# The bias of 739 exps, given as a constant in the instruction instead of by pointer

## The chip, the cores and the metric

The kernel runs on one core of one Trainium2 chip. The metric is the device time of one execution in microseconds (us), the median of several executions. The core has five engines with instruction streams of their own: TensorE (PE in the profile, with its weight loads as PEld), VectorE (DVE), ScalarE (ACT), GpSimd (POOL) and SyncE (SP, which here issues DMA transfers). They meet only at semaphores.

## The reference

Two independent attention blocks with 2048 tokens, width 640 and 32 heads of 20 columns are computed, and their outputs are laid side by side. Block A is softmax attention, block B is linear attention.

```python
# A
scores = jnp.einsum("bhqd,bhkd->bhqk", q, k) * (Dh ** -0.5)
p = _softmax(scores, axis=-1)
o = jnp.einsum("bhqk,bhkd->bhqd", p, v)
# B
phi = lambda t: jnp.where(t > 0, t + 1, jnp.exp(t)) + 1e-6
pq, pk = phi(q), phi(k)
kv = jnp.einsum("bhsd,bhse->bhde", pk, v)
num = jnp.einsum("bhqd,bhde->bhqe", pq, kv)
```

Block A needs 32 x 2048 x 2048 exponentials. Block B needs 2 x 2048 x 640.

## The kernel before, in words

The scores of A are computed transposed, in tiles of 128 keys by 512 queries of one head; one tile is a "unit" and fills one PSUM bank. Eight groups of four heads times four chunks of 512 queries make 32 blocks, each of 16 key tiles times 4 heads.

ScalarE does most of the exponentials. Units are taken in groups of three and two in turn (banks 0 to 2, and banks 3 and 4): `emit_scores` (L1227) issues the score matmuls of group j+1, then `emit_exp` (L1242) issues one ACTIVATE over all banks of group j, so that the scores of one group are computed beside the exp of the other. A group of three is an instruction of 1536 columns, a group of two one of 1024. The result goes as bf16 into the ring `f_PT` of 20 units, from where `emit_pv` (L1368) takes four at a time as moving data of the matmuls with V. In all there are 739 such exps.

VectorE does the remaining units of A by a polynomial on the bits of the number (L1286, L1297, L1301, L1305, into `f_PD`). That form gives the exponential times two to the power 42 (`OCT = 42`) times a small correction (`EXP_S`). ScalarE's exps must carry the same factor, because both kinds of unit are summed together, and it cancels in the normalization. So they add (42 + EXP_S) ln 2 = 29.11 to the exponent: `bias=self.ebias[:, 0:1]`, a column of 128 fp32 numbers in SBUF, which GpSimd fills once at the start (L1035). The scale, 20 to the power -1/2, is a constant in the instruction.

ScalarE has 52 more exps, those of block B (L1554, in `phi`), with scale 1 and bias 0; these carry no tile for the bias. The projections of A, the whole of B, the normalization and the output projections are issued between the exps as background steps.

The order of all instructions on all engines is fixed when the program is built, by a planner (`_Clock`, L728) that keeps an estimated time for each engine. It books `0.062 + 0.4267 * n` us for an exp of n units (L1254), so 1.342 and 0.915 us, and adds a margin `LAG = 0.2` us before results of VectorE and GpSimd count as ready. `bg` (L981) issues background matmuls until TensorE's estimated end reaches the exp's estimated end. `zeros` (L1189) and `fill` (L1208) add matmuls with a zero operand (`f_z`, `f_g`), which change no sum, and whose only effect is that TensorE stays occupied: `fill` does so as long as TensorE's occupied share in the last `SPAN = 3.41` us, weighted by the part of the array that is used, is below `FLOOR = 1.45` us.

Of the kernel before, what the change touches and what calls it, by code (L numbers as in the profile page):

```python
# [5 lines left out]
F32 = mybir.dt.float32  # L6
# [718 lines left out]
LN2 = 0.6931471805599453  # L725
# [74 lines left out]
class _Fast:  # L800
# [53 lines left out]
    def alloc(self):  # L854
        S, NT = self.S, self.NT
        self.KT = self.sb("f_KT", [128, 2, S], BF16)
        self.Qr = self.sb("f_Qr", [128, 4, 512], BF16)
        self.V = self.sb("f_V", [128, NT, N_HEADS, 21], BF16)
        self.xT = self.sb("f_xT", [128, N_DC, S], BF16)
        self.wA = self.sb("f_wA", [128, N_DC, 3 * D_MODEL], BF16)  # L860
        self.wo = self.wA[:, :, 2 * D_MODEL:3 * D_MODEL]
        self.wo7 = self.sb("f_wo7", [128, D_MODEL], BF16)
        self.PT = self.sb("f_PT", [128, self.NPT, 512], BF16)
        self.PD = self.sb("f_PD", [128, self.NPD, 512], BF16)
        self.W = self.sb("f_W", [128, 2, 1024], F32)
        self.PL = self.sb("f_PL", [128, 2, 1024], F32)
        self.T1 = self.sb("f_T1", [128, 512], F32)
        self.Tn = self.sb("f_Tn", [128, 512], BF16)
        self.OTp = self.sb("f_OTp", [128, 512], BF16)
        self.R = self.sb("f_R", [128, 32], F32)  # L870
        self.OTd = self.sb("f_OTd", [128, N_DC, S], BF16)
        self.stage = self.sb("f_st", [128, 4, D_MODEL], BF16)
        self.wBq = self.sb("f_wBq", [128, N_DC, D_MODEL], BF16)
        self.wBkv = self.sb("f_wBkv", [128, N_DC, 2 * D_MODEL], BF16)
        self.woB = self.wBkv[:, :, 0:D_MODEL]
        self.pqT = self.wBkv[:, :, D_MODEL:D_MODEL + 512]
        self.xBt = self.sb("f_xB", [128, 2, N_DC, 512], BF16)
        self.xB = [self.xBt[:, k] for k in range(2)]
        self.kvm = self.sb("f_kvm", [128, N_DC, 21 * N_HEADS], BF16)
        self.kvx = self.sb("f_kvx", [128, 2688 + 10 * 168 + 5 * 168], BF16)  # L880
        self.va = self.kvx[:, 0:2688].rearrange("p (t h j) -> p t h j", t=4, j=21)
        self.kvacc = self.kvx[:, 2688:4368].bitcast(F32).rearrange("p (c n) -> p c n", c=N_DC)
        self.mask = self.kvx[:, 4368:5208].rearrange("p (c n) -> p c n", c=N_DC)
        self.part = self.kvx[:, 0:5120].bitcast(F32).rearrange("p (k n) -> p k n", k=8)
        self.pko = self.sb("f_pk", [128, 4 * D_MODEL], BF16)
        self.pk = self.pko[:].rearrange("p (t n) -> p t n", t=4)
        self.o = self.pko[:, 0:2 * D_MODEL].rearrange("p (t n) -> p t n", t=2)
        self.oT = self.pko[:, 2 * D_MODEL:4 * D_MODEL].rearrange("p (t c m) -> p t c m", t=2, c=N_DC)
        self.ex = self.sb("f_ex", [128, 2, 512], F32)
        self.r1 = self.sb("f_r1", [128, 2, 512], F32)  # L890
        self.rd = self.sb("f_rd", [128, 2, 2, 16], F32)
        self.Z = self.sb("f_z", [128, 128], BF16)
        self.G = self.sb("f_g", [128, 128], BF16)
        self.ebias = self.sb("f_eb", [128, 1], F32)
        self.gmx = self.sb("f_gmx", [128, 2], F32)
        self.ident = self.sb("f_id", [128, 128], BF16)
        self.flag = self.sb("f_flag", [128, 1], I32)
        self.bmx = self.sb("f_bmx", [128, 1], F32)
        self.warm = self.sb("f_warm", [128, 1], F32)
        self.ones = self.sb("f_ones", [128, 1], F32)  # L900
# [115 lines left out]
    def start_loads(self):  # L1016
        sch = self.sch
        awq = self.Aw.rearrange("(c p) n -> p c n", p=128)
        x2 = self.Ax[0]
        xn = self.stage  # L1020
        M = D_MODEL
        for k in range(2):
            sch.dma("sp", lambda e, k=k: e.dma_start(
                xn[:, 2 * k:2 * k + 2, :], x2[256 * k:256 * (k + 1), :].rearrange("(t p) d -> p t d", p=128)),
                writes=tuple(("xn", t) for t in (2 * k, 2 * k + 1)), cost=(0.1, 3.5))
        parts = ((0, 92, ("wq", 0)), (M, M + 92, ("wk", 0)), (2 * M, 2 * M + 160, ("wv", 0)),
                 (M + 92, 2 * M, ("wk", 1)), (92, M, ("wq", 1)), (2 * M + 160, 3 * M, ("wv", 1)))

        def load(q, part):
            a, b, res = part  # L1030
            sch.dma(q, lambda e: e.dma_start(self.wA[:, :, a:b], awq[:, :, a:b]), writes=(res,),
                    cost=(0.5, 5.0 if b - a < 200 else 8.0))
        sch.op("dve", lambda e: e.memset(self.warm[:], 0.0), writes=("warm",))
        sch.op("dve", lambda e: e.memset(self.OTp[:], 1.0), writes=("OTp",), cost=0.3)
        sch.op("pool", lambda e: e.memset(self.ebias[:], (self.OCT + self.EXP_S) * LN2), writes=("ebias",), cost=0.1)  # L1035
        sch.op("act", lambda e: e.activation(self.warm[:], self.warm[:], AF.Exp), writes=("warm",), cost=1.5)
        load("act", parts[0])
        load("act", parts[1])
        load("sp", parts[2])
        for tc in range(1, self.NQC):  # L1040
            for c in range(N_DC):
                sch.dma("sp", lambda e, c=c, tc=tc: e.dma_start_transpose(
                    self.xT[:, c, 512 * tc:512 * (tc + 1)], x2[512 * tc:512 * (tc + 1), 128 * c:128 * (c + 1)]),
                    writes=(("xT", c, tc),), cost=(1.65, 2.0))
        for part in parts[3:]:
            load("sp", part)
# [195 lines left out]
    def emit_exp(self, j):  # L1242
        sch, ps = self.sch, self.ps
        grp = self.groups[j]
        b0 = self.SB[j % 2][0]
        u0 = self.ustart[j]
        s0 = u0 % self.NPT
        n = len(grp)
        assert u0 + n - 1 - self.NPT < 4 * self.pvnext
        scale = float(D_HEAD) ** -0.5  # L1250
        sch.op("act", lambda e: e.activation(self.PT[:, s0:s0 + n, :], ps[:, b0:b0 + n, :], AF.Exp,  # L1251
                                             bias=self.ebias[:, 0:1], scale=scale),
               reads=tuple(("ps", b0 + k) for k in range(n)) + ("ebias",),
               writes=tuple(("PT", s0 + k) for k in range(n)), cost=0.062 + 0.4267 * n)  # L1254

    def d_ready(self, slack):
# [773 lines left out]
```

## Time and profile before

| what | value |
|---|---|
| median of 3 executions | 968.85 us (965.14 to 972.59) |
| the profiled execution's own time | 971.29 us |
| its span, first to last instruction | 969.1 us |
| mean granted TensorE clock | 0.932 of full |
| ScalarE busy | 930.4 us, 96% of the span |
| TensorE busy | 789.4 us, 81% |
| VectorE busy | 718.5 us, 74% |
| GpSimd busy | 160.0 us, 17% |

Busy time is the union of an engine's records. Records of neighbouring instructions on ScalarE overlap, so a record's length is not the time that the instruction costs the engine; that time is the distance from one start to the next. "Idle before" is the time between the end of the records before and the start, and what is named behind it is what ended the wait.

### The profile page before, as it was taken

To read this page: it belongs to the slowest core of one execution; us is meant where nothing else is said; L and a number is where in the kernel's file an instruction comes from. 1 tells how busy PE (TensorE), PEld (TensorE's weight loads), DVE (VectorE), ACT (ScalarE), POOL (GpSimd) and SP (SyncE) were. 2 spreads that over 40 slices of the span, in tenths; PEclk is the share of its full clock that TensorE was granted. 3 is DMA by queue.
4 is the path that set the end of the run, shared out by engine and by line. 5 is a ranking of instruction groups with operands and counts; after the bars stand their busy time and mean duration, and the time that the engine had idled before them with its cause. 6 is when DMAs were issued, how large, how long until landed. Compare 5 with 4: busy or idle time off the path is not lost.

```text
span 969.1 us, 24342 instructions
## 1 busy us (share of the span) xinstructions
PE 789.4 (81%) x10943; PEld 244.1 (25%) x10943; DVE 718.5 (74%) x1003; ACT 930.4 (96%) x799; POOL 160.0 (17%) x154
## 2 busy tenths in 40 slices
PE   8888878777888978787787888887878878878886
PEld 3322222122122222222223122222222222223332
DVE  6768876678789686578885877777887588765773
ACT  6999999999999999999997999999999999999996
POOL 3011301000023121222120320014000310130000
PEclk9989899999889799999998789999998999999999
DMA  6900010000100100100003000010000100000011
GB/s 126 248 5 4 5 32 4 2 5 5 38 5 11 22 5 5 32 5 1 5 5 68 2 3 5 19 43 8 1 12 18 39 6 23 11 5 25 26 40 65
DMA packets 45742, 23.93 MB, mean 25 GB/s; under 512 B 33984, under 2 KB 44992, under 8 KB 45632
## 3 DMA queue, kind: packets, MB, share of 16 engines
q1 hardware_dynamic: 44176, 21.92, 9.6%
q8 instruction: 87, 1.43, 0.6%
q10 hardware_dynamic: 1456, 0.40, 0.2%
q14 instruction: 23, 0.19, 0.1%
HBM read 7.31 MB, written 5.24 MB: 13 GB/s over the span
## 4 chain that ended last, share of the span: by engine, by line
ACT 82%; PE 14%; issue 2%; DVE 1%; ACTq 0%; DVEq 0%
ACT f_PT L1251 80%; PE ps L179 14%; ACT f_ex L1554 2%; DVE f_r L1550 0%; DVE f_W L1286 0%; DVE f_T L1399 0%; DVE f_PL L1301 0%; DVE f_OTp L1416 0%; PE ps L1064 0%; ACT f_st L1528 0%; DVE f_PD L1305 0%; DVE f_PL L1297 0%; PE ps L1702 0%; DVE f_KT L1153 0%; DVE f_Tn L1412 0%
## 5 line engine op out<-in xcount | busy, mean ns | idle before, releaser
L1251 ACT ACTIVATE f_PT<-ps,f_eb 128x1536 bf16<-128x1536 f32 x739 | 917.3, 1468 | 23.9 <-PE ps L179 23.6
L179 PE MATMUL ps<-f_Qr,f_KT 20*128 20x512 bf16 x2048 | 318.5, 406 | 164.8 <-ACT f_PT L1251 150.0
L1286 DVE TENSOR_SCALAR f_W<-ps 128x512 f32<-128x512 f32 x200 | 138.1, 690 | 117.6 <-PE ps L179 115.7
L179 PE MATMUL ps<-f_g,f_z 32*128 32x512 bf16 (+1 forms) x837 | 221.3, 414 | 0.0
L179 PE MATMUL ps<-f_PT,f_V 128*21 128x512 bf16 x1848 | 194.5, 410 | 0.7 <-ACT f_PT L1251 0.7
L179 PEld LDWEIGHTS ps<-f_Qr,f_KT 20*128 20x128 bf16 x2048 | 75.0, 91 | 453.7 <-ACT f_PT L1251 416.1
L1305 DVE SCALAR_TENSOR_TENSOR f_PD<-f_PL,f_W 128x1024 uint16<-128x1024 f32 x100 | 126.2, 1262 | 0.7
L1301 DVE SCALAR_TENSOR_TENSOR f_PL<-f_W,f_PL 128x1024 f32<-128x1024 uint16 x100 | 125.8, 1258 | 0.6
L1297 DVE SCALAR_TENSOR_TENSOR f_PL<-f_W 128x1024 f32<-128x1024 uint16 x100 | 124.7, 1250 | 0.5
L179 PE MATMUL ps<-f_xT,f_wA 128*32 128x512 bf16 x1280 | 110.9, 419 | 0.0
L1409 POOL TENSOR_TENSOR f_Tn<-f_T,f_R 128x320 bf16<-128x320 f32 x31 | 40.1, 1292 | 422.1 <-DVE f_R L1406 422.1
L1557 POOL TENSOR_SCALAR f_ex<-f_ex 128x320 f32<-128x320 f32 (+1 forms) x52 | 45.2, 870 | 347.7 <-ACT f_ex L1554 347.7
L179 PEld LDWEIGHTS ps<-f_PT,f_V 128*21 128x21 bf16 x1848 | 45.7, 89 | 115.7 <-issue 113.5
L179 PE MATMUL ps<-f_wBkv,f_xB 128*32 128x320 bf16 x1280 | 74.0, 324 | 0.0
L179 PEld LDWEIGHTS ps<-f_g,f_z 32*128 32x128 bf16 (+1 forms) x837 | 51.0, 94 | 8.6 <-issue 8.0
L1550 DVE TENSOR_SCALAR f_r<-ps 128x320 f32<-128x320 f32 (+1 forms) x52 | 29.0, 558 | 14.5 <-PE ps L179 14.3
L179 PEld LDWEIGHTS ps<-f_xT,f_wA 128*32 128x32 bf16 x1280 | 30.4, 99 | 31.2 <-issue 19.7
L179 PEld LDWEIGHTS ps<-f_wBkv,f_xB 128*32 128x32 bf16 x1280 | 31.6, 100 | 23.3 <-issue 13.6
L1559 POOL TENSOR_TENSOR f_pk<-f_ex,f_r 128x320 bf16<-128x320 f32 x32 | 36.6, 1142 | 2.7
L179 PE MATMUL ps<-f_wBkv,f_pk 128*32 128x320 bf16 x640 | 35.3, 318 | 0.0
L179 PE MATMUL ps<-f_xB,f_wBq 128*32 128x512 bf16 x400 | 34.3, 406 | 0.0
L179 PE MATMUL ps<-f_wA,f_xT 128*32 128x160 bf16 (+1 forms) x640 | 33.3, 306 | 0.3
(80 smaller groups left out, 490.1 us busy)
## 6 DMA issues: line engine op xcount, KB each, us to landing
out_dram<-f_st SPq DMA_DIRECT2D x31, 160.0 KB
f_OTd<-f_OTp SPq DMA_DIRECT2D x108, 20.0 KB
f_wBkv<-in_B_wqkv_dram SPq DMA_DIRECT2D x1, 1600.0 KB
f_wA<-in_A_wqkv_dram SPq DMA_DIRECT2D x2, 685.0 KB
f_wBq<-in_B_wqkv_dram SPq DMA_DIRECT2D x1, 800.0 KB
f_wA<-in_A_wo_dram SPq DMA_DIRECT2D x1, 800.0 KB
f_wBkv<-in_B_wo_dram SPq DMA_DIRECT2D x1, 800.0 KB
f_st<-in_A_x_dram SPq DMA_DIRECT2D x2, 320.0 KB
```

The source lines that it names most:

```text
L179: lambda e: e.matmul(out, lhsT, rhs, start=start, stop=stop, tile_position=tp, skip_group_check=sgc),
L1251: sch.op("act", lambda e: e.activation(self.PT[:, s0:s0 + n, :], ps[:, b0:b0 + n, :], AF.Exp, bias=self.ebias[:, 0:1], scale=scale), reads ...
L1286: self.dve(0.69, lambda e: e.tensor_scalar(dst, ps[:, b, :], cs, cb, op0=ALU.mult, op1=ALU.add), reads=(("ps", b),), writes=(("W", x, h),))
L1297: self.dve(1.29, lambda e: e.scalar_tensor_tensor(pl, lo, self.EXP_A, lo, op0=ALU.add, op1=ALU.mult), reads=rw, writes=(("PL", x),), fill= ...
L1301: self.dve(1.29, lambda e: e.scalar_tensor_tensor(pl, lo, self.EXP_B, pl, op0=ALU.add, op1=ALU.mult), reads=rw, writes=(("PL", x),), fill= ...
L1305: self.dve(1.29, lambda e: e.scalar_tensor_tensor(pd, pl, self.EXP_K, w, op0=ALU.mult, op1=ALU.add), reads=rw + (("PL", x),), writes=(("PD ...
L1409: sch.op("pool", lambda e: e.tensor_tensor(n3[:, :, 0:D_HEAD], t3[:, :, 0:D_HEAD], rb, op=ALU.mult), reads=("T1", ("R", n % 2)), writes=(" ...
L1550: self.dve(0.16 + 0.00104 * n, lambda e: e.tensor_scalar(r1, src, 0.0, 1e-6, op0=ALU.max, op1=ALU.add), reads=(("ps", b),), writes=(("r1", ...
L1554: sch.op("act", lambda e: e.activation(ex, src, AF.Exp), reads=(("ps", b),), writes=(("ex", k),), cost=0.05 + 0.00084 * n)
L1557: sch.op("pool", lambda e: e.tensor_scalar(ex, ex, 1.0, 0.0, op0=ALU.min, op1=ALU.max), writes=(("ex", k),), cost=0.1 + 0.0019 * n)
L1559: self.done[key] = sch.op("pool", lambda e: e.tensor_tensor(dst, ex, r1, op=ALU.add), reads=(("ex", k), ("r1", k)), writes=(res,), cost=0. ...
```

## The change

The column `f_eb`, GpSimd's memset that fills it and the dependency on it are removed, and the 739 exps take the number itself as bias. The number is the same.

```diff
-        self.ebias = self.sb("f_eb", [128, 1], F32)
...
-        sch.op("pool", lambda e: e.memset(self.ebias[:], (self.OCT + self.EXP_S) * LN2), writes=("ebias",), cost=0.1)
...
         sch.op("act", lambda e: e.activation(self.PT[:, s0:s0 + n, :], ps[:, b0:b0 + n, :], AF.Exp,
-                                             bias=self.ebias[:, 0:1], scale=scale),
-               reads=tuple(("ps", b0 + k) for k in range(n)) + ("ebias",),
+                                             bias=(self.OCT + self.EXP_S) * LN2, scale=scale),
+               reads=tuple(("ps", b0 + k) for k in range(n)),
                writes=tuple(("PT", s0 + k) for k in range(n)), cost=0.062 + 0.4267 * n)
```

The planner's cost for the exp is the same in both kernels, so the order is the same: TensorE, VectorE, ScalarE and SyncE have the same instructions in the same sequence with the same waits, and GpSimd has one memset less.

## The prediction

> **What bounds the kernel now.** I read the page first: the busy times, the granted clock in 40 slices, and the chain of work that ended last.
>
> ```profile
> span 969.1 us, 24342 instructions
> PE 789.4 (81%) x10943; PEld 244.1 (25%) x10943; DVE 718.5 (74%) x1003; ACT 930.4 (96%) x799; POOL 160.0 (17%) x154
> ...
> PEclk9989899999889799999998789999998999999999
> ...
> ACT 82%; PE 14%; issue 2%; DVE 1%; ACTq 0%; DVEq 0%
> ACT f_PT L1251 80%; PE ps L179 14%; ACT f_ex L1554 2%; DVE f_r L1550 0%; DVE f_W L1286 0%; DVE f_T L1399 0%; DVE f_PL L1301 0%; DVE f_OTp L1416 0%; PE ps L1064 0%; ACT f_st L1528 0%; DVE f_PD L1305 0%; DVE f_PL L1297 0%; PE ps L1702 0%; DVE f_KT L1153 0%; DVE f_Tn L1412 0%
> ```
>
> ScalarE (ACT) is busy for 96% of the span, and the chain that set the end lies on it for 82%, nearly all in the exps of line 1251. TensorE carries 14%. Its granted clock is mostly at 9 tenths, with slices at 7 and 8. Next come the waits, in total us, times and longest.
>
> ```profile
> PE ps L179 <- ACT f_PT L1251: 150.7, 346, 1.5
> DVE f_W L1286 <- PE ps L179: 115.7, 151, 4.5
> ACT f_PT L1251 <- PE ps L179: 23.6, 39, 3.8
> ```
>
> TensorE stands waiting for an exp to free its banks 346 times (150.7 us). The other way round, the exps wait for scores only 39 times (23.6 us). So ScalarE paces the kernel, except in a few places. Those places show in windows that I laid on the 25 stretches before the tail in which the granted clock was half. The columns are the window, its length, busy us (and records) of PE, PEld, DVE, ACT and POOL, the clock, and DMA.
>
> ```profile
> 59.80:63.20 3.40, 3.40 (x31) 0.63 (x27) 3.21 (x4) 3.40 (x4) 1.31 (x2) 0.50 0.01 2
> ...
> 759.50:762.90 3.40, 3.40 (x31) 0.75 (x31) 0.00 (x0) 3.40 (x4) 2.35 (x3) 0.50 0.22 51
> sum 129.30, PE 124.56 PEld 29.55 DVE 85.64 ACT 112.96 POOL 30.32; mean PE 4.98 PEld 1.18 DVE 3.43 ACT 4.52 POOL 1.21
> ```
>
> In these 129.3 us TensorE is busy for 124.56, so there it sets the pace. ScalarE has 16.3 us of idle records there, out of 23.6 for its waits on scores in the whole span.
>
> How much ScalarE loses in all needs the price of one exp. Records overlap, so I use the distance from one start to the next, in the timeline of ScalarE (start, length, instructions merged).
>
> ```profile
> 303.47 0.48 ACT L1554 ACTIVATE f_ex<-ps 128x320 f32<-128x320 f32 x1
> 303.79 7.47 ACT L1251 ACTIVATE f_PT<-ps,f_eb 128x1024 bf16<-128x1024 f32 x6
> 311.05 0.54 ACT L1554 ACTIVATE f_ex<-ps 128x320 f32<-128x320 f32 x1
> ...
> 655.76 3.63 ACT L1251 ACTIVATE f_PT<-ps,f_eb 128x1024 bf16<-128x1024 f32 x3
> 659.17 0.70 ACT L1554 ACTIVATE f_ex<-ps 128x512 f32<-128x512 f32 x1
> 659.65 11.40 ACT L1251 ACTIVATE f_PT<-ps,f_eb 128x1536 bf16<-128x1536 f32 x9
> 670.75 0.79 ACT L1554 ACTIVATE f_ex<-ps 128x512 f32<-128x512 f32 x1
> 671.23 3.75 ACT L1251 ACTIVATE f_PT<-ps,f_eb 128x1024 bf16<-128x1024 f32 x3
> ```
>
> Line 1554 takes no tile for the bias, and line 1251 takes `f_eb`. After an exp of line 1554 with 320 columns the next start comes 303.79 - 303.47 = 0.32 us later. After one with 512 columns it comes 0.48 us later (659.17 to 659.65, 670.75 to 671.23). The difference of 0.16 us over 192 columns is 0.833 ns a column, which leaves a **fixed part of 0.053 us**. For line 1251, six exps take 311.05 - 303.79 = 7.26 us with 7680 columns (3 x 1024 and 3 x 1536). The columns account for 6.40, so 0.86 / 6 = 0.143 remains for each. Nine exps take 670.75 - 659.65 = 11.10 us with 11776 columns, or 1.29 / 9 = 0.143. Three take 659.17 - 655.76 = 3.41 us with 3584 columns, or 0.142. So the **fixed part of an exp with the pointer is 0.143 us**.
>
> ```profile
> L1251 ACT ACTIVATE f_PT<-ps,f_eb 128x1536 bf16<-128x1536 f32 x370 | 621.8, 1680 | 18.4 <-PE ps L179 18.3
> L1251 ACT ACTIVATE f_PT<-ps,f_eb 128x1024 bf16<-128x1024 f32 x369 | 462.7, 1254 | 5.5 <-PE ps L179 5.4
> L1554 ACT ACTIVATE f_ex<-ps 128x320 f32<-128x320 f32 x32 | 17.3, 539 | 0.2 <-DVE f_r L1550 0.2
> L1554 ACT ACTIVATE f_ex<-ps 128x512 f32<-128x512 f32 x20 | 14.9, 747 | 0.1
> L1077 ACT COPY f_xT<-ps 128x512 bf16<-128x512 bf16 x2 | 1.1, 588 | 4.2 <-PE ps L1064 4.2
> ...
> L1251 ACT ACTIVATE f_PT<-ps,f_eb x739: 1104/1540/1979, 10.9 to 957.4; 128x1536 bf16<-128x1536 f32 x185
> ```
>
> From the first exp's start to the last one's are 946.5 us. In them lie 370 x 1536 + 369 x 1024 columns, and 32 x 320 + 20 x 512 of block B. That is 966,656 columns at 0.833 ns, or 805.2 us. The fixed parts are 739 x 0.143 = 105.7 and 52 x 0.053 = 2.8. Less 1.4 for the last exp, whose time lies behind its start, this is 912.3, so **about 34 us are lost to late scores**, somewhat more than the idle records show, since each wait also hides the overlap.
>
> **The change, part by part.** 1. The exps' fixed part. The trace of before has no exp with a constant bias other than zero. The two kinds that it has differ in three things: pointer or constant, bf16 or fp32 out, and width. The width is taken out above. For the bf16 output there is a copy at the start:
>
> ```profile
> 6.44 1.07 ACT L1077 COPY f_xT<-ps 128x512 bf16<-128x512 bf16 x2 [4.20 <-PE ps L1064]
> ```
>
> Two copies take 1.07 us and one takes 0.588 (above), so their starts are 0.48 us apart. With 512 columns that leaves 0.055 us, with bf16 out and no pointer. So the output type isn't the 0.09 us; what is left is the pointer. Bounds: 0.143 us (nothing gained) and 0.053 us (both rows without a pointer). The new form is nearest to line 1554, the same function from PSUM with a constant bias, so I take 0.053. That gives 739 x 0.09 = **-66.5 us** on the engine that sets the end.
>
> The Trainium skill, page "ScalarE: Activation LUTs", section "What ACT_TABLE_LOAD costs", prices each pointer operand at about 93 ns and says that neighbouring ACTIVATEs overlap by the same 93 ns. By its price the sum would be 739 x 0.093 = 68.7 us. If its overlap were what hides the pointer's read, it would be nothing. The fixed 0.143 us between starts, where the overlap is already counted, speaks for the first.
>
> 2. The memset and its dependency.
>
> ```profile
> 0.73 0.10 POOL L1035 MEMSET f_eb<- 128x1 f32 x1 [0.29 <-POOLq L2015]
> ```
>
> GpSimd fills the column at 0.73 us, and the first exp starts at 10.9. That exp waits for its scores until then. Without the memset GpSimd's queue starts 0.1 us earlier, with work that nothing near needs: 0 us. No order, wait or DMA changes elsewhere, so no queue has a new neighbour.
>
> 3. What is late next, at full clock. The exps come 6.9% closer, and TensorE and VectorE must fit the same work in. The last long stretch at full clock shows what there is:
>
> ```profile
> 773.80:957.00 183.20, 152.92 (x2336) 53.00 (x2336) 131.07 (x210) 183.20 (x155) 20.77 (x18) 1.00 0.06 21
> ```
>
> ```profile
> PE ps L179 <- ACT f_PT L1251: 27.7, 64, 1.0
> ```
>
> ScalarE is never idle there, and TensorE waits for it for 27.7 us. The change takes about 150 exps x 0.09 = 13.5 us away, half of that wait. VectorE's fullest slice of 40 us is this one:
>
> ```profile
> 280.00:320.00 40.00, 32.49 (x430) 9.67 (x422) 34.62 (x43) 39.56 (x37) 10.53 (x10) 0.93 0.11 22
> ```
>
> Its 34.62 us must fit in 37.2. So both engines have room on average, but a group of scores is computed only one exp ahead, and TensorE's waits are uneven. The bounds for new waits are 0 and 13 us (the need of this stretch, once); nearer to the first, since the wait there is twice the need. I take **+3 us**.
>
> 4. The half-clock stretches. In them TensorE sets the pace, so faster exps win nothing. ScalarE's 113 us there are 93 exps at the mean distance of 1.21 us, 8.4 us of the 66.5. But how many of the stretches remain? The 3.4 us ahead of each of the 25, of which the lowest and the highest in TensorE's busy time and the sum are shown:
>
> ```profile
> 247.50:250.90 3.40, 1.81 (x27) 0.34 (x19) 2.79 (x4) 3.40 (x4) 0.38 (x1) 1.00 0.00 0
> ...
> 428.40:431.80 3.40, 2.54 (x35) 0.78 (x39) 2.22 (x3) 3.40 (x5) 1.32 (x2) 1.00 0.07 18
> ...
> sum 85.00, PE 54.56 PEld 15.73 DVE 61.82 ACT 84.19 POOL 15.63; mean PE 2.18 PEld 0.63 DVE 2.47 ACT 3.37 POOL 0.63
> ```
>
> TensorE is busy for 54.56 of 85.0 us there, 64% against 81% in the whole span and 83% in the quiet stretch above, while ScalarE is busy for 84.19. So the clock falls behind thin stretches that the exps pace, and those are what the change packs. The exps' mean distance goes from 1.21 to 1.12 us, so such a stretch gets 8% more of TensorE's work. Of the 25, whose mean is 2.18 us, eleven lie below 2.18; with 8% more they stay below 2.36, where 21 of the 25 lie now. The others come above it, where the clock falls in only 4 of these rows. The kernel's own filling with zero matmuls is planned with exps of 1.342 and 0.915 us; the trace has 1.42 and 1.00. So it comes 7% too thin now, and about 1% too dense after. So I take 11 of 25 stretches as left. Their gaps are between 16 us (idle inside them) and the 34 us of all; I take 25. Fourteen of 25 gone gives **-14 us**; in the eleven left, 11 / 25 x 8.4 = **+3.7 us** of the saving is not won.
>
> **Sum.** 969.1 - 66.5 + 3 - 14 + 3.7 = 895.3 us span. The profiled execution took 2.2 us more than its span (971.29), so 897.5; it lies 0.25% above the median of the runs shown, so **895 us** against 968.85.
>
> **The rivals.** *All half-clock stretches stay.* Where the clock falls may follow the background work alone. For it: the stretches lie at places of particular work, with TensorE full in them. Against: the 84.19 us of ScalarE just ahead. Span 969.1 - 66.5 + 8.4 + 3 = 914, the median the same within 0.2.
>
> *The stretches all go.* 969.1 - 66.5 - 25 + 3 = 880.6, so 880. For it: the planner's distances then hold nearly exactly. Against: the 64% become 69%, still far below the 81%. The Trainium skill, "TensorE: Matmul & The Clock Gate", Part 1 (the HAM clock gate), says that activity in a free-running window of 3.4 us releases a default half rate. By that rule denser work can only shorten the stretches; the lengths here, 3.4 us in the first and the last of the rows above, agree.
>
> *TensorE or VectorE takes over at full clock.* The exps would then wait for scores in most groups, and half of the 58 us left outside the stretches is lost: 969.1 - 66.5 + 29 - 7 = 924, where 7 is what the sum above has for the stretches and the small waits. For it: VectorE's 34.62 of 37.2, TensorE's 346 waits against 739 exps. Against: the 27.7 us above.
>
> *The constant costs what the pointer did.* Then the 0.09 us belong to something else that the two kinds of exp differ in, and the time stays at 969. Against: the copy.
>
> *Slower.* Faster exps could make TensorE's work bunch, so that more windows are thin and the half clock spreads. A us of half clock costs now 25 / 129.3 = 0.19 us, and after, with the 8.4 us not won, 0.26. The 66.5 us are eaten from 256 us more of half clock on, 385 in all; at 430 us the time is 981. Against: the same matmuls in a shorter time.
>
> **How the numbers follow.** The forecast, with some 6 to 18 of the stretches left, 62% (886 to 905). All stay: 14%. All go: 12%. TensorE or VectorE takes over: 5%. No change: 4%. Slower: 3%. The range 880 to 914 takes in the first three but for their edges; it leaves out the 12% of the others and some 6% of the edges. About 1% either way is what a measurement of this kernel can tell from no change (its three times spread by 0.8%). Faster by more than that: 0.93; within: 0.04; slower: 0.03.
>
> **What would show it.** Right: the start-to-start distances of the exps at full clock come to 1.33 and 0.91 us (now 1.42 and 1.00), and the order is unchanged; the mean granted clock rises above 0.932; TensorE's 150.7 us of waiting for exps falls towards 90; the exps' waits for scores stay below 24 us. Wrong: distances unchanged (the pointer wasn't it), or distances as said but the exps' waits for scores at 40 us and more. In that case the granted clock tells whether half-clock stretches (more of them) or TensorE's and VectorE's own work at full clock took the gain.

## The result

| | before | changed |
|---|---|---|
| median | 969.79 us (965.14 to 972.59) | 899.07 us (897.15 to 900.43) |
| the profiled execution's own time | 971.29 us | 900.43 us |
| its span | 969.1 us | 898.4 us |
| mean granted TensorE clock | 0.932 | 0.971 |

The kernel before was executed once more beside the changed one, so its median is now of four. The ratio is 0.927, with a 95% interval of 0.923 to 0.932. The forecast was 895 us, with a range of 880 to 914.

The page of the changed kernel, with the same parts as shown of before: busy times, granted clock, and the chain that ended last.

```profile
span 898.4 us, 24341 instructions
...
PE 758.1 (84%) x10943; PEld 242.5 (27%) x10943; DVE 715.6 (80%) x1003; ACT 864.3 (96%) x799; POOL 163.7 (18%) x153
...
PEclk9999999999999989999997799999899999999999
...
ACT 84%; PE 10%; DVE 4%; issue 2%; ACTq 0%; DVEq 0%
```

ScalarE (ACT) still sets the pace. Its busy time fell by 66 us, the span by 70.7. TensorE's (PE) share of the chain fell from 14% to 10%, VectorE's (DVE) rose from 1% to 4%. TensorE's own busy time fell by 31 us with the same instructions in the same order: its clock was full more of the time. The waits, in total us, times and longest:

```profile
PE ps L179 <- ACT f_PT L1249: 116.2, 302, 1.5
DVE f_W L1284 <- PE ps L179: 74.1, 100, 3.7
ACT f_PT L1249 <- PE ps L179: 16.6, 21, 3.9
```

TensorE waits less for the exps (150.7 before), and the exps wait less for scores (23.6 before), although they come faster. The distances between starts, in ScalarE's timeline (start, length, instructions merged):

```profile
524.94 12.38 ACT L1249 ACTIVATE f_PT<-ps 128x1024 bf16<-128x1024 f32 x11
537.01 0.81 ACT L1552 ACTIVATE f_ex<-ps 128x512 f32<-128x512 f32 x1
537.48 63.61 ACT L1249 ACTIVATE f_PT<-ps 128x1536 bf16<-128x1536 f32 x56
600.67 0.92 ACT L1552 ACTIVATE f_ex<-ps 128x512 f32<-128x512 f32 x1
```

Eleven exps take 537.01 - 524.94 = 12.07 us with 13,824 columns (6 x 1024 and 5 x 1536). At 0.833 ns that is 11.52, so 0.55 / 11 = **0.050 us** remains as the fixed part; it was 0.143. The next 56 take 63.19 us with 71,680 columns, and there 3.48 / 56 = 0.062 us remains, though ScalarE has no idle record among them. I come back to those 12 ns.

The half-clock stretches, laid out as in the prediction (window, length, busy us of PE, PEld, DVE, ACT and POOL, clock, DMA):

```profile
57.50:60.90 3.40, 3.40 (x31) 0.61 (x31) 3.31 (x4) 3.36 (x4) 1.42 (x2) 0.51 0.01 2
...
484.20:504.70 20.50, 19.50 (x161) 4.05 (x161) 13.02 (x17) 13.65 (x12) 2.78 (x2) 0.50 0.10 21
...
648.00:651.40 3.40, 3.40 (x44) 1.20 (x41) 2.03 (x4) 2.54 (x3) 0.00 (x0) 0.51 0.01 2
sum 51.10, PE 50.10 PEld 10.60 DVE 38.05 ACT 40.72 POOL 11.95; mean PE 5.57 PEld 1.18 DVE 4.23 ACT 4.52 POOL 1.33
```

Nine stretches are left of 25, and 51 us of 129. One of them is 20 us long.

### The profile page after: what moved, and what is told of

It is laid out like the page before. It is cut to its first block, busy times and chain, and to the rows that moved or that the text cites. A ratio compares the mean times of both kernels' runs of the same rounds, so it can differ in the third digit from the quotient of the medians.

```text
span 898.4 us, 24341 instructions
## 1 busy us (share of the span) xinstructions
PE 758.1 (84%) x10943; PEld 242.5 (27%) x10943; DVE 715.6 (80%) x1003; ACT 864.3 (96%) x799; POOL 163.7 (18%) x153
## 4 chain that ended last, share of the span: by engine, by line
ACT 84%; PE 10%; DVE 4%; issue 2%; ACTq 0%; DVEq 0%
ACT f_PT L1249 81%; PE ps L179 10%; ACT f_ex L1552 3%; DVE f_PL L1295 1%; DVE f_PL L1299 1%; DVE f_PD L1303 1%; DVE f_W L1284 0%; DVE f_r L1548 0%; PE ps L1062 0%; DVE f_OTp L1414 0%; DVE f_T L1397 0%; ACT f_st L1526 0%; DVE f_KT L1155 0%; DVE f_R L1404 0%; DVE f_KT L1151 0%
## 5 line engine op out<-in xcount | busy, mean ns | idle before, releaser
L1249 ACT ACTIVATE f_PT<-ps 128x1536 bf16<-128x1536 f32 x739 | 853.7, 1452 | 17.2 <-PE ps L179 16.6
L179 PE MATMUL ps<-f_Qr,f_KT 20*128 20x512 bf16 x2048 | 310.2, 393 | 123.7 <-ACT f_PT L1249 115.6
L179 PE MATMUL ps<-f_g,f_z 32*128 32x512 bf16 (+1 forms) x837 | 214.2, 399 | 0.0
L179 PE MATMUL ps<-f_PT,f_V 128*21 128x512 bf16 x1848 | 187.6, 395 | 0.5 <-ACT f_PT L1249 0.5
L179 PE MATMUL ps<-f_xT,f_wA 128*32 128x512 bf16 x1280 | 105.3, 401 | 0.1
L179 PE MATMUL ps<-f_wBkv,f_xB 128*32 128x320 bf16 x1280 | 68.5, 302 | 0.1
L1557 POOL TENSOR_TENSOR f_pk<-f_ex,f_r 128x320 bf16<-128x320 f32 x32 | 38.4, 1200 | 2.7
L1552 ACT ACTIVATE f_ex<-ps 128x320 f32<-128x320 f32 (+1 forms) x52 | 36.2, 696 | 1.5 <-DVE f_r L1548 1.5
```

The source lines that it names most:

```text
L179: lambda e: e.matmul(out, lhsT, rhs, start=start, stop=stop, tile_position=tp, skip_group_check=sgc),
L1552: sch.op("act", lambda e: e.activation(ex, src, AF.Exp), reads=(("ps", b),), writes=(("ex", k),), cost=0.05 + 0.00084 * n)
L1557: self.done[key] = sch.op("pool", lambda e: e.tensor_tensor(dst, ex, r1, op=ALU.add), reads=(("ex", k), ("r1", k)), writes=(res,), cost=0. ...
```

## The experiments

Each kernel ran on one chip in turn with the kernel before. Since the granted clock of this kernel is either full or half, the time at half clock is 2 x (1 - mean clock) x span; with 0.932 and 969.1 us that is 132 us before, and with 0.971 and 898.4 us it is 52 us after (the tail is in both). Those are the profiled executions. The clock differs from execution to execution: beside the experiments the kernel before ran 29 times, with 87 to 148 us at half clock and 113 us on average, and the changed kernel ten times, with 47 to 67 us and 54 us on average.

### The price of a pointer: three runs

**Scale by pointer, bias constant.** In the changed kernel:

```diff
+        self.escale = self.sb("f_es", [128, 1], F32)
...
+        sch.op("pool", lambda e: e.memset(self.escale[:], float(D_HEAD) ** -0.5), writes=("escale",), cost=0.1)
...
-                                             bias=(self.OCT + self.EXP_S) * LN2, scale=scale),
-               reads=tuple(("ps", b0 + k) for k in range(n)),
+                                             bias=(self.OCT + self.EXP_S) * LN2, scale=self.escale[:, 0:1]),
+               reads=tuple(("ps", b0 + k) for k in range(n)) + ("escale",),
```

> The changed kernel with one edit: the exps' scale comes from a column in SBUF, by pointer, and the bias stays a constant. Theory (each pointer operand costs the exp about 0.093 us between starts): the exps' distances go back to 1.42 and 1.00 us, and the time to that of before, 969 us (960 to 978). Rival (it is something of the bias alone, its path or its dependency): the distances stay at 1.33 and 0.90 us and the time at 899 us.

It took 973.58 us (965.22 to 976.96), 1.002 of before, interval 0.998 to 1.007. ScalarE's timeline:

```profile
661.85 11.40 ACT L1251 ACTIVATE f_PT<-ps,f_es 128x1536 bf16<-128x1536 f32 x9
672.95 0.79 ACT L1554 ACTIVATE f_ex<-ps 128x512 f32<-128x512 f32 x1
```

Nine exps take 11.10 us, to the hundredth what the same nine took with the bias by pointer. So the price is not one of the bias or its path alone: a pointer for the scale costs the same. This run has a dependency on a memset too, so it leaves open whether that is the price; the third run settles it.

**Both by pointer.** In the kernel before, the same column for the scale as above, with its dependency:

```diff
-                                             bias=self.ebias[:, 0:1], scale=scale),
+                                             bias=self.ebias[:, 0:1], scale=self.escale[:, 0:1]),
```

> The kernel before with the scale by pointer too, so two pointers in each of the 739 exps. Theory (a price for each pointer): distances of 1.52 and 1.09 us, 739 x 0.093 = 68 us on top of 969, so 1037 us, and some more, up to 1050, because TensorE's work gets thinner and its clock falls to half more often. Rival (the pointers are read side by side, one price for any number): 969 us.

It took 1036.44 us (1031.74 to 1041.51), 1.070 of before, interval 1.065 to 1.076. That is 67 us above before, the price of the second pointer (739 x 0.093 = 69); the up to 13 us that were expected of the clock on top did not come.

```profile
594.14 14.37 ACT L1253 ACTIVATE f_PT<-ps,f_eb,f_es 128x1024 bf16<-128x1024 f32 x11
608.26 0.74 ACT L1556 ACTIVATE f_ex<-ps 128x512 f32<-128x512 f32 x1
```

Eleven exps take 14.12 us with 13,824 columns, which leaves 0.237 us each. So the fixed part is 0.050, 0.143 and 0.237 us with none, one and two pointers: **0.093 us for each pointer, and they add up**.

**Pointer in one width alone.** In the kernel before:

```diff
-                                             bias=self.ebias[:, 0:1], scale=scale),
+                                             bias=self.ebias[:, 0:1] if n == 3 else (self.OCT + self.EXP_S) * LN2, scale=scale),
```

> The pointer only in the 370 exps of 1536 columns, the constant in the 369 of 1024. Theory (a fixed price for each instruction, whatever its width): distances of 1.42 and 0.90 us, 370 x 0.093 = 34 us above the changed kernel, so 933 us (928 to 940). Rival (the price falls where a constant form and a pointer form follow each other, or belongs to one width): 899 or 969 us.

It took 936.12 us (935.67 to 939.96), 0.965 of before, interval 0.963 to 0.968; the forecast was 933.

```profile
646.12 1.74 ACT L1251 ACTIVATE f_PT<-ps,f_eb 128x1536 bf16<-128x1536 f32 x1
647.54 0.80 ACT L1554 ACTIVATE f_ex<-ps 128x512 f32<-128x512 f32 x1
...
650.35 1.26 ACT L1251 ACTIVATE f_PT<-ps 128x1024 bf16<-128x1024 f32 x1
651.25 0.84 ACT L1554 ACTIVATE f_ex<-ps 128x512 f32<-128x512 f32 x1
```

The wide form with the pointer holds the engine for 1.42 us, the narrow one with the constant for 0.90. The two forms take turns here and keep their prices. The `reads` line is unchanged in this run, so the narrow exps kept the dependency on the memset and yet lost the 0.093 us: the price is the pointer's, not the dependency's. About half of the exps gave about half of the gain (33 of 70 us).

### The half clock: eight runs

**The planner told the true cost, in the kernel before.**

```diff
-               writes=tuple(("PT", s0 + k) for k in range(n)), cost=0.062 + 0.4267 * n)
+               writes=tuple(("PT", s0 + k) for k in range(n)), cost=0.143 + 0.4267 * n)
```

> The kernel before with the planner's cost of an exp put to what the profile shows with the pointer, 0.143 + 0.4267 n instead of 0.062 + 0.4267 n. Theory of the half-clock stretches (there are 25 of them because the order is planned for exps that are 7% shorter than they are): with the true cost they fall to about 10, as in the changed kernel, and the time to 955 us (950 to 962). Rival (the stretches follow the background work, not the planned distance): some 25 stretches and 969 us.

It took 964.69 us (961.29 to 966.80), 0.9945 of before, interval 0.992 to 0.997, and so above the range of 950 to 962. The mean clock of its profiled execution and its waits:

```profile
core 0: 963.3 us, clock 0.961
```

```profile
ACT f_PT L1251 <- PE ps L179: 17.7, 25, 2.1
```

A mean clock of 0.961 is 2 x 0.039 x 963 = 75 us at half clock, in 14 stretches before the tail, where about 10 were expected and the rival had 25. The exps' waits for scores are 17.7 us (23.6 before). For the time the executions beside each other are the fair comparison: on average 106 us at half clock in the eleven of the kernel before, 81 in the six of this one. Those 25 us at the prediction's 0.19 give the 5 us that the time fell. So the planned distance that was too short caused a part of the stretches, and the forecast of 14 us counted on more of them than it did. The order is another one here, and the planner, told the true cost, also adds 145 zero matmuls, so the distance and the filling are not told apart.

**No filling.** In the changed kernel, `FLOOR = 1.45` becomes `FLOOR = 0.0`, which leaves out `fill`'s 264 zero matmuls and none of the results. It does one thing more: `bg`, which issues the background matmuls, tests the same bound, and with 0.0 it stops earlier. So the order of the rest changes as well.

> The changed kernel without the filling with four full matmuls of zeros (FLOOR 0 instead of 1.45; it changes no sum). Theory (the clock falls behind thin windows, and ScalarE loses about 0.26 us for each us of half clock): half clock rises from 51 us in 9 stretches to 200 us or more, and the time to 899 + 0.26 x 150 = 938 us (920 to 955). Rival (the half-clock stretches follow the background work, the filling is of no use): 899 us or a little less.

It took 923.16 us (921.97 to 925.04), 0.950 of before, interval 0.945 to 0.955.

```profile
core 0: 923.1 us, clock 0.917
```

```profile
ACT f_PT L1249 <- PE ps L179: 38.4, 62, 2.8
```

Half clock is 2 x 0.083 x 923 = 153 us, 101 more than in the changed kernel, and the time is 24 us more: 0.24 us for each us of half clock, where the prediction had 0.26 (the changed order is in this figure; the last section has one without it). The exps wait for scores 62 times instead of 21. Half clock had been expected to reach 200 us, so the time is at the low end of the range given. The rival, that the filling is of no use, falls, though what `fill` and what `bg` did is not told apart.

**More filling.** `FLOOR` becomes 1.6, then, beside the changed kernel on one chip, 1.6 again, 1.75 and 1.9.

> The changed kernel with more filling (FLOOR 1.6 instead of 1.45). Theory (as above): at most 4 half-clock stretches besides the long one of 20 us at 484 us, and the time falls by 30 us x 0.26 = 8 us, to 891 (888 to 896). Rival (more zero matmuls stand in the way of the scores): the exps' waits for scores grow at full clock, 899 us or more.

It took 893.82 us (892.43 to 900.97), 0.919 of before, interval 0.915 to 0.924. The profiled execution is the one of 900.97 us, with a clock of 0.972 and eight half-clock stretches, where at most five were expected; the other four have a clock of 0.986 to 0.990.

> The changed kernel once more, beside the next three on the same chip: 899 us (895 to 904). Theory and rivals agree; it is the measure for the others.

> FLOOR 1.6, again, beside the changed kernel. Theory (more filling keeps the clock up): 894 us, 4 to 7 us below the changed kernel on the same chip, at a higher granted clock. Rival (the 894 us were the other chip): no difference.

> FLOOR 1.75. Theory: another step up in the clock, to 0.985 and more, and 889 to 893 us. Rival (the zero matmuls begin to delay the scores): the clock rises and the time does not, 894 us or more, with longer waits of the exps at full clock.

> FLOOR 1.9. Theory: hardly any half clock left besides the tail, 886 to 892 us. Rival (the zero matmuls delay the scores): 895 us or more at the highest clock of all.

| FLOOR | median, us | range | ratio to before | mean clock of the six executions |
|---|---|---|---|---|
| 1.45 (the changed kernel) | 900.30 | 897.20 to 902.47 | 0.9295 (0.9268 to 0.9321) | 0.969 (0.963 to 0.972) |
| 1.6 | 895.59 | 891.35 to 901.15 | 0.9244 (0.9208 to 0.9281) | 0.986 (0.978 to 0.993) |
| 1.75 | 896.72 | 891.31 to 899.82 | 0.9247 (0.9214 to 0.9280) | 0.988 (0.981 to 0.995) |
| 1.9 | 905.35 | 901.86 to 915.03 | 0.9369 (0.9329 to 0.9409) | 0.980 (0.968 to 0.986) |

More filling raises the clock up to 1.6 and hardly beyond, so the next steps down that were expected of 1.75 and 1.9 did not come. The two settings of 1.6 and 1.75 are 4 to 5 us below the changed kernel in the median, but the intervals overlap: a gain of half a per cent is likely and not established. At 1.9 the clock is above that of the changed kernel and the time is longer, with intervals apart. The rival's time came there, but not the highest clock of all. The waits of TensorE at FLOOR 1.9:

```profile
PE ps L179 <- ACT f_PT L1249: 76.4, 243, 1.0
PE ps L179 <- DVE f_PD L1303: 13.8, 7, 4.1
```

TensorE's slack for the exps falls to 76 us (116 in the changed kernel). Its waits for VectorE's exponentials (`f_PD`) are 1.6 us in all in the changed kernel, 6 at 1.6, 9 at 1.75 and 14 here (and 6 without filling, so the order has a part in them). The exps' own waits for scores are 20.3 us against 16.6, though the clock is higher. That the zero matmuls themselves delay the scores fits with this, but this run changes the whole order, so what exactly cost the time stays open.

**The planner told the true cost, in the changed kernel:** `cost=0.050 + 0.4267 * n`.

> The changed kernel with the planner's cost of an exp put to what the profile shows with the constant, 0.050 + 0.4267 n instead of 0.062 + 0.4267 n. Theory (the planned distance matters as the true one does): the order gets 0.5 to 1% less dense against the plan's own clock and the same against the true one; half clock and time stay within 1%, 895 to 903 us. Rival (the plan is at its best where it is a little too slow): more late scores, 905 us or more.

It took 907.41 us (900.61 to 911.65), 0.935 of before, interval 0.930 to 0.941. That is what the rival gave, but the interval overlaps with the 0.923 to 0.932 of the changed kernel, which ran on another occasion. The true cost is at least no better than one that is 12 ns too long.

### The long stretch

The 20 us stretch of the changed kernel begins behind a gap. TensorE's timeline there, and then the same place before:

```profile
480.80 0.34 PE L179 MATMUL ps<-f_wA 128*32 128x32 bf16 x27
485.20 0.29 PE L179 MATMUL ps<-f_wA 128*32 128x32 bf16 x13 [4.06 <-issue]
```

```profile
522.27 0.34 PE L179 MATMUL ps<-f_wA 128*32 128x32 bf16 x27
526.67 0.29 PE L179 MATMUL ps<-f_wA 128*32 128x32 bf16 x13 [4.06 <-issue]
```

In both kernels TensorE stands still for 4.06 us after the same instruction, within a run of its smallest matmuls. The four other traces with this order have the gap at the same instruction, with 3.3 to 4.1 us. A run spread the small matmuls out:

```diff
                     if i == 3 and c == N_DC - 1:
-                        yield 300
+                        yield 1200
```

> The changed kernel with the planner's charge for twenty of the smallest matmuls (32 columns, the step that decides on the bound for the flag) raised from 300 to 1200 columns, so that they are spread between other work instead of standing in runs of 60 to 100. Theory (in the changed kernel as before it TensorE stands still for 4.06 us inside such a run, waiting for nothing that the profile shows, then runs at half clock for 20 us, and ScalarE loses some 14 us there): the gap goes, and the time falls by 8 to 14 us, to 885 to 891. Rival (the gap comes wherever these matmuls are): a gap of 4 us elsewhere and 899 us.

It took 903.76 us (898.37 to 908.18), 0.932 of before, interval 0.926 to 0.937, so nothing was won. The gap is gone, but the new order has another one:

```profile
682.22 0.39 PE L179 MATMUL ps<-f_PD,f_V 128*21 128x512 bf16 x2
687.88 0.60 PE L179 MATMUL ps<-f_PD,f_V 128*21 128x512 bf16 x2 [5.27 <-DVE f_PD L1303]
```

Here TensorE waits 5.27 us for VectorE's exponentials. Neither the theory's time nor the rival's gap at the same matmuls came out. In the changed kernel the gap coincides with a burst of transfers (the window 480.80 to 484.20 has 235 GB/s on the DMA engines):

```profile
480.80:484.20 3.40, 0.34 (x31) 0.23 (x23) 0.00 (x0) 1.35 (x1) 0.00 (x0) 1.00 1.48 235
```

That TensorE's instructions were late behind these transfers is a guess that was not tried by itself. The run above doesn't settle it: in the changed kernel 140 of the 520 small matmuls run beside five transposing loads (478.5 to 485.4 us), and in that run the loads come at 523.7, after the last of them, so it parted the two as well as spreading the matmuls. And at FLOOR 1.9, 100 of them run beside the loads without such a gap. The cause stays open. It bears little on the change and its gain, since both kernels have the gap.

## Why the prediction was right

**1. The fixed part: right.** The step gave -66.5 us from 0.09 us for each of 739 exps. The traces give 0.143 - 0.050 = 0.093, so -68.7 us. The prediction read 0.053 off starts rounded to hundredths of a us. The Trainium skill's price in "ScalarE: Activation LUTs", section "What ACT_TABLE_LOAD costs", about 93 ns for each pointer operand, is what the runs show, for either operand and for both together. The other reading, that an overlap of the same size hides the pointer between neighbours, falls with the distances themselves.

**2. The memset: right.** GpSimd's stream is one instruction shorter and the first exp starts no earlier (11.4 us against 10.9):

```profile
L1249 ACT ACTIVATE f_PT<-ps x739: 1018/1445/1830, 11.4 to 886.5; 128x1536 bf16<-128x1536 f32 x185
```

**3. New waits at full clock: right in kind, too small.** From the first exp's start to the last one's are 875.0 us. The columns take 805.2 us and the fixed parts 739 x 0.050 + 52 x 0.050 = 39.6, less 1.3 for the last exp. So some 31 us are lost, against 34 before: 3 us less, where the prediction had 7 less (+3 - 14 + 3.7). How they divide can be read exp by exp from the traces with this order. What a distance has beyond its columns and fixed part is counted to the half clock when the distance touches a half-clock stretch:

| trace | lost at half clock, us | lost at full clock, us |
|---|---|---|
| two pointers | 26 | 1 |
| one pointer: before, scale by pointer | 31, 31 | 3, 4 |
| pointer in half of the exps | 27 | 9 |
| none: changed, once more | 19, 16 | 12, 13 |

The closer the exps come, the more is lost at full clock: the term of +3 us was +9. A third of that rise has no idle record: 265 exps at full clock start 8 to 25 ns later than the fixed part allows (4.0 us in sum), against 62 before (1.0 us). They make the 0.062 us in the stretch of 56 above. Why they are of this size the trace does not tell. The long quiet stretch at the end shows the room:

```profile
651.40:886.00 234.60, 205.03 (x3064) 69.84 (x3060) 181.36 (x278) 234.20 (x214) 31.64 (x28) 1.00 0.08 23
400.00:440.00 40.00, 32.89 (x464) 9.98 (x460) 36.90 (x47) 40.00 (x40) 10.22 (x9) 1.00 0.02 4
```

```profile
PE ps L179 <- ACT f_PT L1249: 27.1, 66, 0.9
PE ps L179 <- DVE f_PD L1303: 0.4, 2, 0.2
```

TensorE still waits for the exps 66 times in the first of these windows, to which the two waits belong. VectorE's fullest slice, the second, rose from 34.62 to 36.90 of 40 us, or 92%, where 34.62 of 37.2 foresaw 93%. It shows in the chain (4%), but it did not take over.

**4. The half-clock stretches: right, and in part by luck.** Eleven were expected, nine came. The loss in them fell by 12 us (31 to 19 in the table); the prediction had -14 + 3.7 = -10.3. Since the time at half clock differs so much between executions, nine against eleven is no sharp agreement. Seven of the nine lie at matmuls where a stretch lay before, two at others. And one of the nine, with 20 of the 51 us, is the one behind the gap, which the step doesn't have. The 3.4 us ahead of the stretches now read:

```profile
330.60:334.00 3.40, 2.27 (x35) 0.72 (x35) 3.35 (x4) 3.40 (x4) 0.00 (x0) 1.00 0.00 0
...
480.80:484.20 3.40, 0.34 (x31) 0.23 (x23) 0.00 (x0) 1.35 (x1) 0.00 (x0) 1.00 1.48 235
...
sum 30.60, PE 19.27 PEld 5.48 DVE 24.02 ACT 28.38 POOL 6.73; mean PE 2.14 PEld 0.61 DVE 2.67 ACT 3.15 POOL 0.75
```

But for the gap (0.34), TensorE is busy for 2.25 us or more in each of them, 2.37 on average. Before, more than half lay below 2.25, down to 1.81. These rows are only the windows behind which the clock fell; the prediction looked at no others. In each trace the stretches begin whole multiples of 3.41 us apart, so both spans can be cut into windows on that grid. Of the windows at full clock before the tail:

| TensorE busy in the window, us | before: windows, clock fell behind | changed: windows, clock fell behind |
|---|---|---|
| under 2.25 | 21, 16 | 3, 1 |
| 2.25 to 2.6 | 70, 9 | 47, 8 |
| over 2.6 | 153, 0 | 196, 0 |

So the thin windows were packed out of the range in which the clock falls, as the step said. Its bound was too sharp, though: between 2.25 and 2.6 us the clock mostly holds and sometimes falls, so the busy time alone doesn't decide it, and three of the rows left lie above the 2.36 that the step gave them. The runs with the planner's cost and with the filling point the same way. So do those with this order: the time at half clock averages 190 us in the executions with two pointers, 113 with one, 88 with the pointer in half of the exps and 54 with none. The Trainium skill's rule ("TensorE: Matmul & The Clock Gate", Part 1), that activity in a window of 3.4 us releases the half rate, agrees with these.

**The sum.** Fixed part -68.6 (738 x 0.093, up to the last exp's start), half clock -12, full clock +9, and +0.8 at both ends of the span: -71, for 969.1 to 898.4. The prediction had -73.8. Its error of 3.1 us in the span is the full-clock term (+5.9) and the ends (+0.8), less what the half clock (-1.5) and the fixed part (-2.1) gave beyond their steps. So it is as small as it is because errors of both signs met; the fixed part alone is 97% of the gain.

**What was to show it.** Distances of 1.33 and 0.90 us, a higher clock and fewer waits for scores came. TensorE's wait for the exps was to fall towards 90 us and fell to 116: the prediction took the exps' gain off it, but forgot that a faster clock gives TensorE idle time back (its busy time fell by 31 us).

**The rivals.** *All stay* and *all go*: nine of 25 left. *TensorE or VectorE takes over*: not at this distance, as step 3 shows. *The constant costs what the pointer did*: refuted by the distances. *Slower*: half clock fell where that needed it to spread.

## What to carry to other kernels

Where ScalarE sets the pace with many short ACTIVATEs, count the pointer operands: a `[128, 1]` column of equal numbers costs 0.093 us in each instruction, here 7% and 9% of exps that held the engine for 1.42 and 1.00 us, and a constant costs none of it. Read such a price from the distance of one start to the next, between forms that differ in little, since the records' lengths (1,680 ns before and 1,664 after for the wide exp) hide it. An engine that becomes faster can also thicken another's work and so its clock; that gave 12 us more here, of which new waits at full clock took 9 back. Where the order is planned, the planner's cost should be looked at together with the change.

## What was not expected of the hardware

The record of the wide exp hardly changed: 1,680 ns before, 1,664 ns after, while its hold on the engine fell from 1.423 to 1.330 us. Groups of ScalarE in the changed kernel:

```profile
L1249 ACT ACTIVATE f_PT<-ps 128x1536 bf16<-128x1536 f32 x370 | 615.7, 1664 | 11.9 <-PE ps L179 11.7
L1249 ACT ACTIVATE f_PT<-ps 128x1024 bf16<-128x1024 f32 x369 | 457.1, 1239 | 5.2 <-PE ps L179 5.0
L1552 ACT ACTIVATE f_ex<-ps 128x320 f32<-128x320 f32 x32 | 20.5, 641 | 0.2 <-DVE f_r L1548 0.2
```

The exps of block B did not change, and their records grew from 539 to 641 ns: the records overlap more when the instructions come closer, so a mean length says next to nothing of the cost of an instruction here.

Executions of one and the same kernel differ in the granted clock, and the time follows it. The six of FLOOR 1.6 run from 891.35 us at a clock of 0.993 to 901.15 us at 0.979. So within one kernel the spread of about 1% is largely the half clock too. This also prices it with the order held fixed: in the 29 executions of the kernel before the time rises by 0.17 us for each us at half clock (correlation 0.94), in the ten of the changed kernel by 0.27 (0.80). The prediction had 0.19 and 0.26.
